# Two gated linear-attention blocks: the first four k chunks, and the transfers of x and of the first key weights, put in another order

## The chip, the core and the metric

The kernel runs on one core of a Trainium2 chip. The metric is the device time of one execution in microseconds (us), as the median of several runs. TensorE (PE) does the matmuls and the transposes, VectorE (DVE) and ScalarE (ACT) work on their results, GpSimd (POOL) builds masks, and SyncE (SP) issues most of the transfers from DRAM; ScalarE issues some.

## The reference

Two linear-attention blocks, A and B, read the same x (2048 x 640) with their own weights, and a gate mixes them:

```
g   = sigmoid((x * gate_w).sum(-1))
qkv = x @ wqkv                              # 640 x 1920, 32 heads of 20
phi = where(t > 0, t + 1, exp(t)) + 1e-6
kv  = sum over s of phi(k)[s] v[s]          # 20 x 20 for each head
o   = phi(q) kv / (phi(q) . sum phi(k))
out = g * (oA @ woA) + (1 - g) * (oB @ woB)
```

## The kernel before

x is worked in 16 chunks of 128 rows. The model dimension of 640 is five row blocks of 128 (c = 0 to 4). A **k chunk** is phi(k) for one chunk of x: for each of two halves of 320 columns, five matmuls (one for each c) add up in PSUM; the stationary operand is the chunk of x transposed (`xT[:, c, chunk]`), the moving one is row block c of the key weights (`wkA`). `k_done` then runs `phi` (L188): exp on ScalarE, two steps on VectorE, the result in `pk`. A **q block** (`q_block`, L244) is 20 matmuls of 512 columns with the query weights `wqA` stationary and xT moving, and phi again.

After the k chunks and q blocks of A come its gate, its sums over x and phi(k), its normalisation, then the same for B, and at last the products with the output weights. These stages lie behind the change and are not touched by it.

PSUM is four tiles (slots 0 to 3) that are used in turn; a tile can be written again when the work that reads it is done. `turn[0]` is the slot that comes next, unless a slot is named.

What decides the order at the start:

- Each engine takes its instructions in the order in which the program has them. TensorE begins with seven warm-up matmuls (L151) on constants.
- x chunks 0 to 3 come from DRAM as rows (`xn`) and are transposed on TensorE (`x_transpose`, L181: five transposes into PSUM, then one copy of 640 columns to `xT` on VectorE or ScalarE). The other twelve chunks come already transposed by 15 transposing loads on SP (L123), five for each group of four chunks.
- Loads are issued on two queues, SP's and ScalarE's. SP's has x chunk 0, row blocks 0, 2 and 4 of wkA, then wqA (one load of 800 KB, L119) and the transposing loads. ScalarE's has x chunk 1, row blocks 1 and 3 of wkA, then x chunks 2 and 3 in one load. A row block and an x chunk are 160 KB each.
- `k_first` (L216) does the first two k chunks side by side, block by block: transposes of chunks 0 and 1; blocks 0 and 1 for chunk 0, then for chunk 1 (8 matmuls); block 2 for both (4); block 3 for both (4); block 4 for chunk 0 (2); the transposes of chunks 2 and 3; block 4 for chunk 1 (2). Their sums lie in slots 2 and 3, and both phis are called at the end.
- The main loop (L636) goes on with k chunks 2 and 3 (slots 0 and 1, 10 matmuls each), the q blocks of the first 512 rows (slots 2 and 3), k chunks 4 to 7, and so on.

Of the kernel before, what the change touches and what calls it, by code (L numbers as in the profile page):

```python
# [8 lines left out]
P = 128  # L9
# [5 lines left out]
S, D, H = 2048, 640, 32  # L15
Dh = D // H
DT = D // P
ST = S // P
NB = 4
CB = 4  # L20
# [10 lines left out]
def kernel(  # L31
# [11 lines left out]
    nc = tc.nc  # L43
# [10 lines left out]
    turn = [0]  # L54

    def ps_raw(name, slot=None):

        if slot is None:
            slot = turn[0]
            turn[0] = (slot + 1) % 4  # L60
        return psum.tile([P, 4 * HB], BF16, tag=f"ps{slot}", name=name)

    def ps(name, slot=None):

        return ps_raw(name, slot).bitcast(FP32).rearrange("p (b n) -> p b n", b=2)

    xT = persist.tile([P, DT, S], BF16, name="xT")
# [27 lines left out]
    wq_dram = [A_wqkv.rearrange("(c p) f -> p c f", p=P), B_wqkv.rearrange("(c p) f -> p c f", p=P)]  # L95
# [7 lines left out]
    wk = [None, None]  # L103
# [3 lines left out]
    def load_x(eng, lo, hi):  # L107
        eng.dma_start(out=xn[:, lo:hi, :], in_=xb0[:, lo:hi, :])

    def load_wk(eng, c):  # L110
        eng.dma_start(out=wk[0][:, c, :], in_=wq_dram[0][:, c, D:2 * D])

    load_x(nc.sync, 0, 1)
    load_x(nc.scalar, 1, 2)
    for c in range(DT):
        load_wk(nc.scalar if c % 2 else nc.sync, c)
    load_x(nc.scalar, 2, 4)
    wq[0] = wpool.tile([P, DT, D], BF16, tag="wq", name="wqA")
    nc.sync.dma_start(out=wq[0][:], in_=wq_dram[0][:, :, 0:D])  # L119
# [1 line left out]
    for n in range(1, NB):  # L121
        for c in range(DT):
            nc.sync.dma_start_transpose(  # L123
                out=xT[:, c, n * HB:(n + 1) * HB], in_=x2[n * HB:(n + 1) * HB, c * P:(c + 1) * P]
# [8 lines left out]
    for sign, base in ((1, 0), (-1, Dh - 1)):  # L133
        nc.gpsimd.affine_select(
            out=maskE[:], in_=maskE[:], pattern=[[sign * P, DT], [-sign * Dh, H]],
# [3 lines left out]
    for r in range(4):  # L139
        rows = slice(32 * r, 32 * r + 32)  # L140
        for sign, base in ((1, 0), (-1, Dh - 1)):
            nc.gpsimd.affine_select(
                out=E4[rows], in_=E4[rows], pattern=[[sign, D]],
# [34 lines left out]
            nc.scalar.activation(out=ge[b][:], in_=pt[:, 0, :], func=ACT.Exp, scale=(-1.0, 1.0)[b])  # L178
            nc.vector.tensor_scalar(ge[b][:], ge[b][:], 1.0, 1e30, op0=ALU.add, op1=ALU.min)

    def x_transpose(i, slot, eng):  # L181
        pt = ps_raw("xt", slot)
        for c in range(DT):
            nc.tensor.transpose(out=pt[:, c * P:(c + 1) * P], in_=xn[:, i, c * P:(c + 1) * P], identity=ident[:])
        copy = nc.scalar.copy if eng == "act" else nc.vector.tensor_copy
        copy(out=xT[:, :, i * P:(i + 1) * P], in_=pt[:, 0:D].rearrange("p (c n) -> p c n", c=DT))

    def phi(dst, src, n, lifted=False):  # L188

        e = work.tile([P, 2, n], BF16, tag="e", name="e", bufs=3)  # L190
        nc.scalar.activation(out=e[:], in_=src, func=ACT.Exp)  # L191
        if lifted:
            nc.scalar.activation(out=dst, in_=src, func=ACT.Identity, bias=lift[:])
        nc.vector.tensor_scalar(e[:], e[:], 1.0, EPS, op0=ALU.min, op1=ALU.add)  # L194
        if lifted:
            nc.vector.tensor_tensor(out=dst, in0=dst, in1=e[:], op=ALU.max)
            return
        nc.vector.scalar_tensor_tensor(out=dst, in0=src, scalar=1.0 + EPS, in1=e[:], op0=ALU.add, op1=ALU.max)  # L198

    def k_mm(b, i, c, pt, hf):  # L200
        nc.tensor.matmul(  # L201
            pt[:, hf, 0:HF], lhsT=xT[:, c, i * P:(i + 1) * P], rhs=wk[b][:, c, hf * HF:(hf + 1) * HF],
            start=(c == 0), stop=(c == DT - 1),
        )

    def k_done(b, i, pt):
        phi(pk[:, i, :].rearrange("p (b n) -> p b n", b=2), pt[:, :, 0:HF], HF)

    def k_chunk(b, i):
        pt = ps(f"k{'AB'[b]}")  # L210
        for hf in range(2):
            for c in range(DT):
                k_mm(b, i, c, pt, hf)
        k_done(b, i, pt)

    def k_first():  # L216

        for i in range(2):
            x_transpose(i, i, "dve")
        pts = [ps("kA", 2 + i) for i in range(2)]  # L220
        for cs in ((0, 1), (2,), (3,), (4,)):
            for i in range(2):
                for c in cs:
                    for hf in range(2):
                        k_mm(0, i, c, pts[i], hf)
                if cs[0] == DT - 1 and i == 0:
                    x_transpose(2, 0, "dve")
                    x_transpose(3, 1, "act")
        for i in range(2):
            k_done(0, i, pts[i])  # L230

    def q_unit(b, m, h, lifted=False):
# [11 lines left out]
    def q_block(b, m, n):  # L244

        pt = ps(f"q{'AB'[b]}")
        for u in range(2):
            for c in range(DT):
                nc.tensor.matmul(  # L249
                    pt[:, u, :], lhsT=wq[b][:, c, (m + u) * P:(m + u + 1) * P], rhs=xT[:, c, n * HB:(n + 1) * HB],  # L250
                    start=(c == 0), stop=(c == DT - 1),
                )
        phi(pqT[b][:, m:m + 2, n * HB:(n + 1) * HB], pt, HB)
# [378 lines left out]


    k_first()
    turn[0] = 0
    for n in range(2):  # L636
        for i in range(max(2, n * CB), (n + 1) * CB):
            k_chunk(0, i)
        for m in (0, 2):
            q_block(0, m, n)  # L640
# [3 lines left out]
    for n in range(1, NB):  # L644
        nc.sync.dma_start(
            out=xn[:, n * CB:(n + 1) * CB, :], in_=x2[n * HB:(n + 1) * HB, :].rearrange("(q p) d -> p q d", p=P)
# [36 lines left out]
    with tc.manual_schedule():  # L683
# [15 lines left out]
        with late_pool("single") as single:  # L699
            halves = [[bank(single, f"s{c}{hf}") for hf in range(2)] for c in (3, 4)]  # L700
            for c in (3, 4):
                pts = [t[:, 0:HF] for t in halves[c - 3]]
# [16 lines left out]
        for i in range(1, half):  # L719
            p, after = pairs[i], pairs[i + 1] if i + 1 < half else None  # L720
# [45 lines left out]
```

## Time and profile before

| | us |
|---|---|
| median of 3 runs | 197.63 |
| lowest and highest | 197.43, 198.44 |
| the profiled execution | 198.14 |
| its span in the profile | 196.4 |
| first k matmul (L201) starts | 5.11 |
| first q matmul (L249) starts | 12.40 |
| TensorE work of the chain ends | 190.09 |

Busy times of the page are shares of the span; a wait is the idle time of an engine before an instruction, and the name behind the arrow is what ended it. Times on the timeline and in the chain are from the span's start. A time to landing counts from the issue of a transfer until the data is there. PEld is the loading of the stationary operand, which goes on beside matmuls.

### The profile page before, as it was taken

Reading aid. Unit: us, or ns where it says so; the run is one execution under the profiler, and the core shown is the slowest. Engines: PE = TensorE matmul, PEld = TensorE weight load, DVE = VectorE, ACT = ScalarE, POOL = GpSimd, SP = SyncE. Lnnn points to the kernel's source line nnn. Section 1 sums busy time; section 2 is a strip of 40 time slices with the busy share of each in tenths; the row PEclk is TensorE's granted clock in tenths of the full one; section 3 lists DMA queues with packets and bytes.
Section 4 is the critical chain, followed back from the end, with each engine's and each line's share of the span. In section 5 each row is a group of like instructions: output and inputs, shape, how many; then the busy total and the mean of one; then the engine's idle time right before and its main releaser. Section 6 shows DMA issues by size and latency. Waiting matters only on the chain.

```text
span 196.4 us, 3665 instructions
## 1 busy us (share of the span) xinstructions
PE 190.9 (97%) x1513; PEld 122.4 (62%) x1520; DVE 148.8 (76%) x240; ACT 82.4 (42%) x110; POOL 9.3 (5%) x23
## 2 busy tenths in 40 slices
PE   8899999999999999999999999999999999999992
PEld 3456547664476666877764444576667777777771
DVE  4296868898989896888787677768779798885553
ACT  2245455555941874366652554413552520122110
POOL 7920000000000000000000000000000000000000
PEclk9999999999999999999999999999999999999999
DMA  6975469970050000220071000000000002122112
GB/s 174 313 143 83 104 163 373 246 199 4 2 167 3 0 0 3 77 90 3 0 155 38 2 0 0 0 3 0 3 0 0 3 0 100 71 82 78 72 68 69
DMA packets 18189, 14.21 MB, mean 72 GB/s; under 512 B 8782, under 2 KB 18046, under 8 KB 18174
## 3 DMA queue, kind: packets, MB, share of 16 engines
q1 hardware_dynamic: 17566, 13.17, 25.1%
q10 hardware_dynamic: 576, 0.82, 1.2%
q8 instruction: 12, 0.20, 0.4%
q14 instruction: 3, 0.02, 0.1%
q0 software_dynamic: 32, 0.00, 0.0%
HBM read 9.40 MB, written 2.62 MB: 61 GB/s over the span
## 4 chain that ended last, share of the span: by engine, by line
PE 93%; DMA 3%; DVE 1%; issue 0%; SPq 0%; ACT 0%; DVEq 0%; ACTq 0%
PE gB L271 11%; PE kB L201 11%; PE qB L238 11%; PE kA L201 11%; PE gs L297 8%; PE qA L238 7%; PE ox L501 6%; PE oy L501 5%; PE oz L501 5%; PE qA L249 4%; DMA wkA<-in_A_wqkv_dram 3%; PE ow L501 2%; PE gA L271 2%; PE mA L414 1%; DVE osb L506 1%; PE exA L474 1%
## 5 line engine op out<-in xcount | busy, mean ns | idle before, releaser
L201 PEld LDWEIGHTS <-xT 128*128 128x128 bf16 x320 | 30.8, 98 | 14.0 <-issue 1.3
L194 DVE TENSOR_SCALAR e<-e 128x640 bf16<-128x640 bf16 (+1 forms) x52 | 19.2, 369 | 11.1 <-ACT e L191 10.0
L201 PE MATMUL kA<-wkA,xT 128*128 128x320 bf16 x160 | 23.1, 299 | 0.7 <-DMA wkA<-in_A_wqkv_dram 0.6
L271 PEld LDWEIGHTS <-xn 128*128 128x128 bf16 x192 | 18.3, 98 | 8.4 <-issue 1.3
L271 PE MATMUL gB<-pk,xn 128*128 128x320 bf16 x160 | 22.9, 299 | 0.0
L201 PE MATMUL kB<-wkB,xT 128*128 128x320 bf16 x160 | 22.9, 299 | 0.0
L238 PE MATMUL qB<-xT,wqB 128*128 128x512 bf16 x97 | 21.9, 379 | 0.2
L191 ACT ACTIVATE e<-kA 128x640 bf16<-128x640 f32 x16 | 11.3, 704 | 13.5 <-PE kA L201 13.5
L238 PEld LDWEIGHTS <-wqB 128*128 128x128 bf16 x100 | 9.6, 98 | 11.4 <-issue 0.3
L191 ACT ACTIVATE e<-kB 128x640 bf16<-128x640 f32 x16 | 11.3, 705 | 10.7 <-PE kB L201 10.7
L191 ACT ACTIVATE e<-qB 128x1024 bf16<-128x1024 f32 x10 | 10.2, 1024 | 13.1 <-PE qB L238 10.7
L198 DVE SCALAR_TENSOR_TENSOR pk<-kA,e 128x640 bf16<-128x640 f32 x16 | 13.2, 825 | 1.9 <-PE gps L157 0.5
L191 ACT ACTIVATE e<-qA 128x1024 bf16<-128x1024 f32 x10 | 10.2, 1024 | 10.5 <-PE qA L249 5.2
L198 DVE SCALAR_TENSOR_TENSOR pk<-kB,e 128x640 bf16<-128x640 f32 x16 | 13.2, 824 | 1.7
L238 PE MATMUL qA<-xT,wqA 128*128 128x512 bf16 x58 | 13.5, 379 | 0.1
L198 DVE SCALAR_TENSOR_TENSOR pqTB<-qB,e 128x1024 bf16<-128x1024 f32 x10 | 12.2, 1225 | 1.0
L535 ACT COPY u<-ox 128x320 f32<-128x320 f32 x8 | 3.4, 427 | 20.9 <-PE ox L501 20.9
L488 ACT CAST ex<-exA 128x1024 bf16<-128x1024 f32 x10 | 9.6, 1017 | 5.8 <-PE exA L474 4.9
L501 PEld LDWEIGHTS <-xT 128*128 128x128 bf16 x85 | 8.1, 98 | 2.9
L238 PEld LDWEIGHTS <-wqA 128*128 128x128 bf16 x60 | 5.7, 97 | 6.7 <-issue 0.3
L501 PEld LDWEIGHTS <-pqTA 128*128 128x128 bf16 x85 | 8.0, 98 | 2.9
L501 PEld LDWEIGHTS <-pqTB 128*128 128x128 bf16 x80 | 7.8, 98 | 3.0
(118 smaller groups left out, 272.5 us busy)
## 6 DMA issues: line engine op xcount, KB each, us to landing
out_dram<-osb SPq DMA_DIRECT2D x15, 160.0 KB, 1.8
xn<-in_A_x_dram SPq DMA_DIRECT2D x3, 640.0 KB, 5.9
wqA<-in_A_wqkv_dram SPq DMA_DIRECT2D x1, 800.0 KB, 6.8
wvA<-in_A_wqkv_dram SPq DMA_DIRECT2D x1, 800.0 KB, 9.7
wkB<-in_B_wqkv_dram SPq DMA_DIRECT2D x1, 800.0 KB, 4.7
wqB<-in_B_wqkv_dram SPq DMA_DIRECT2D x1, 800.0 KB, 4.8
wvB<-in_B_wqkv_dram SPq DMA_DIRECT2D x1, 800.0 KB, 5.0
woA<-in_A_wo_dram SPq DMA_DIRECT2D x1, 750.0 KB, 12.2
```

What stands on the lines that cost most here:

```text
L191: nc.scalar.activation(out=e[:], in_=src, func=ACT.Exp)
L194: nc.vector.tensor_scalar(e[:], e[:], 1.0, EPS, op0=ALU.min, op1=ALU.add)
L198: nc.vector.scalar_tensor_tensor(out=dst, in0=src, scalar=1.0 + EPS, in1=e[:], op0=ALU.add, op1=ALU.max)
L201: nc.tensor.matmul(pt[:, hf, 0:HF], lhsT=xT[:, c, i * P:(i + 1) * P], rhs=wk[b][:, c, hf * HF:(hf + 1) * HF], start=(c == 0), stop=(c == D ...
L238: nc.tensor.matmul(pt[:, u, :], lhsT=wq[b][:, c, m * P:(m + 1) * P], rhs=xT[:, c, n * HB:(n + 1) * HB], start=(c == 0), stop=(c == DT - 1),)
L249: nc.tensor.matmul(pt[:, u, :], lhsT=wq[b][:, c, (m + u) * P:(m + u + 1) * P], rhs=xT[:, c, n * HB:(n + 1) * HB], start=(c == 0), stop=(c ...
L271: nc.tensor.matmul(pt[:, hf, 0:HF], lhsT=xn[:, i, c * P:(c + 1) * P], rhs=pk[:, i, hf * HF:(hf + 1) * HF], start=(i == 0), stop=(i == ST - 1),
L297: nc.tensor.matmul(pt[:, n, 0:HF], lhsT=left[:, i, n * P:(n + 1) * P], rhs=right[:, i, :], start=(first and i == 0), stop=(i == hc - 1), s ...
L414: nc.tensor.matmul(dst, lhsT=KVT[:rows, j, c * P:(c + 1) * P], rhs=wo_sb[b][:rows, j, hf * HF:(hf + 1) * HF], start=(k == 0), stop=(k == 1),)
L488: nc.scalar.copy(out=ex[:], in_=src)
L501: nc.tensor.matmul(dst, lhsT=left[:, c, r0:r0 + P], rhs=right[:, c, :], start=(first and c == 0), stop=(c == DT - 1), skip_group_check=not ...
L535: nc.scalar.copy(out=self.u2[:], in_=self.at("x"))
```

## The change

wkA's row blocks 2, 3 and 4 come in one transfer of 480 KB on SP's queue; ScalarE's queue has x chunk 1, row block 1 and then x chunks 2 and 3. `x_transpose` can copy to xT in pieces; chunks 0 and 1 are copied as blocks 0 and 1, then blocks 2 to 4. `k_first` does four chunks: blocks 0 and 1 for chunks 0 and 1; the transposes of chunks 2 and 3; block 2 for chunks 0 and 1; blocks 0 and 1 for chunks 2 and 3 (slots 0 and 1); then, chunk by chunk, the blocks that are left, each chunk followed by its phi. The main loop skips the first four chunks and starts with the q blocks in slot 2, as before.

```
-    def load_wk(eng, c):
-        eng.dma_start(out=wk[0][:, c, :], in_=wq_dram[0][:, c, D:2 * D])
+    def load_wk(eng, lo, hi):
+        eng.dma_start(out=wk[0][:, lo:hi, :], in_=wq_dram[0][:, lo:hi, D:2 * D])
 
     load_x(nc.sync, 0, 1)
     load_x(nc.scalar, 1, 2)
-    for c in range(DT):
-        load_wk(nc.scalar if c % 2 else nc.sync, c)
+    load_wk(nc.sync, 0, 1)
+    load_wk(nc.scalar, 1, 2)
+    load_wk(nc.sync, 2, DT)
     load_x(nc.scalar, 2, 4)
...
-    def x_transpose(i, slot, eng):
+    def x_transpose(i, slot, eng, cuts=(0, DT)):
...
-        copy(out=xT[:, :, i * P:(i + 1) * P], in_=pt[:, 0:D].rearrange("p (c n) -> p c n", c=DT))
+        src = pt[:, 0:D].rearrange("p (c n) -> p c n", c=DT)
+        for lo, hi in zip(cuts, cuts[1:]):
+            copy(out=xT[:, lo:hi, i * P:(i + 1) * P], in_=src[:, lo:hi])
...
     def k_first():
 
+        pts = [ps("kA", (2 + i) % 4) for i in (0, 1)]
+
+        def part(i, cs):
+            for c in cs:
+                for hf in range(2):
+                    k_mm(0, i, c, pts[i], hf)
+
         for i in range(2):
-            x_transpose(i, i, "dve")
-        pts = [ps("kA", 2 + i) for i in range(2)]
-        for cs in ((0, 1), (2,), (3,), (4,)):
-            for i in range(2):
-                for c in cs:
-                    for hf in range(2):
-                        k_mm(0, i, c, pts[i], hf)
-                if cs[0] == DT - 1 and i == 0:
-                    x_transpose(2, 0, "dve")
-                    x_transpose(3, 1, "act")
+            x_transpose(i, i, "dve", (0, 2, DT))
         for i in range(2):
+            part(i, (0, 1))
+        x_transpose(2, 0, "dve")
+        x_transpose(3, 1, "act")
+        for i in range(2):
+            part(i, (2,))
+        pts += [ps("kA", i) for i in (0, 1)]
+        for i in (2, 3):
+            part(i, (0, 1))
+        for i in range(4):
+            part(i, (3, 4) if i < 2 else (2, 3, 4))
             k_done(0, i, pts[i])
...
     k_first()
-    turn[0] = 0
+    turn[0] = 2
     for n in range(2):
-        for i in range(max(2, n * CB), (n + 1) * CB):
+        for i in range(CB if n else 0, CB * 2 * n):
             k_chunk(0, i)
```

## The prediction

> **What bounds the kernel now.** I read the page first (busy shares, then the chain that ended last), then the chain in order of time for the first 13 us, then the timeline, the DMA issues and the DMA queues of that stretch. On the page TensorE is busy 97% of the span, and the chain that ended last is 93% TensorE; the one other entry of size is a load.
>
> ```profile
> PE 190.9 (97%) x1513; PEld 122.4 (62%) x1520; DVE 148.8 (76%) x240; ACT 82.4 (42%) x110; POOL 9.3 (5%) x23
> PE 93%; DMA 3%; DVE 1%; issue 0%; SPq 0%; ACT 0%; DVEq 0%; ACTq 0%
> ```
>
> So the end is set by TensorE's stream, and only the time in which TensorE stands still can be won. The chain in order of time shows where that is (start, length, what):
>
> ```profile
> 1.72 5.23 DMA wkA<-in_A_wqkv_dram
> 6.95 0.04 issue
> 7.00 0.70 PE kA L201 x4
> 7.70 0.02 issue
> 7.72 0.97 PE kA L201 x6
> 8.69 0.68 PE xt L184 x10
> 9.37 0.29 PE kA L201 x2
> 9.66 0.02 issue
> 9.68 2.89 PE kA L201 x20
> 12.57 0.22 PE qA L249
> 12.78 0.05 issue
> 12.84 4.05 PE qA L249 x18
> 16.89 5.43 PE kA L201 x40
> ```
>
> wkA's row block 2 lands at 1.72 + 5.23 = 6.95, and from then on the chain is TensorE without a break until the last microseconds. A k matmul costs 5.43 / 40 = 0.136 us; 20 of them cost 2.72 plus 0.16 for the last one to run out (299 ns on the page, less 0.136), which is the 2.89 of the row. The timeline gives the stretch before 6.95 and the waits inside it:
>
> ```profile
> 5.11 1.26 PE L201 MATMUL kA<-wkA,xT 128*128 128x320 bf16 x8
> 7.00 1.70 PE L201 MATMUL kA<-wkA,xT 128*128 128x320 bf16 x10 [0.62 <-DMA wkA<-in_A_wqkv_dram]
> 8.63 0.56 PEld L184 LDWEIGHTS <-xn 128*128 128x128 bf16 x10 [0.28 <-DMA xn<-in_A_x_dram]
> 9.21 3.36 PE L201 MATMUL kA<-wkA,xT 128*128 128x320 bf16 x22
> 12.40 4.48 PE L249 MATMUL qA<-xT,wqA 128*128 128x512 bf16 x19
> ```
>
> Eight matmuls (row blocks 0 and 1, x chunks 0 and 1) start at 5.11; at 0.136 TensorE could take the next at 6.20. The first q matmul starts at 12.40. Between lie 32 matmuls (32 x 0.136 = 4.35) and 10 transposes (0.68): 5.03 us of work in 6.20 us. So **1.17 us** of standing still is all that this change can win: 0.59% of 197.63.
>
> **When data lands.** From issue times and times to landing of single transfers: x chunk 0 at 3.7, x1 at 3.9, row blocks 0 and 1 at 4.6 and 4.7, block 2 at 6.95, block 3 at 7.6, block 4 at 8.2, x chunks 2 and 3 (one transfer) at 8.6. All of them are 1440 KB, and the two queues (q1 holds SP's transfers, q10 ScalarE's) are never empty until then. The answers for 6 to 7 us and 7 to 8 us (packets, MB, share):
>
> ```profile
> q10 hardware_dynamic: 94, 0.19, 51.6%
> q1 hardware_dynamic: 97, 0.11, 39.3%
> ...
> q1 hardware_dynamic: 254, 0.32, 87.1%
> q10 hardware_dynamic: 34, 0.07, 17.0%
> ```
>
> While both have work they move about equally many packets (97 and 94 here; 153 and 162 from 3 to 4 us), and when one runs dry the other gets nearly all. Bytes moved come to 1429 KB at 7.0 us, so the mean engine has everything by then; but the last landings are 8.2 and 8.6, so the slowest engine is over 1 us behind. Landings, not means, are what TensorE waits for.
>
> **The change, part by part.**
>
> *Transfers.* SP issues x0, block 0, then blocks 2 to 4 as one 480 KB transfer; ScalarE issues x1, block 1, then x2 and x3. Bytes are the same, issues are 6 in place of 8. An issue is 0.39 to 0.46 us, so x2 and x3 are issued at 1.7 in place of 2.2; that alone is worth nothing, since q10 holds x1 and block 1 until about 4.7. What counts is that they move one block (160 KB) ahead in q10. Landings in q10 were 480 KB at 7.6 and 800 KB at 8.6; 640 KB lies between, at 8.1 by bytes and, with 448 packets (128 for each 160 KB load; 192 of the 576 are left for x2 and x3) between 384 and 576, at 7.95 by packets. I take **x2 and x3 at 8.0** (bounds: 7.3, a third of a us under block 3's landing, and 8.6, where they land now). Blocks 2 to 4 can be used only when all 480 KB are there. All 1440 KB had landed at 8.6, with 160 KB or more of wqA already mixed in; 8.2 is block 4's landing. I take **8.5** (bounds 7.5 and 9.0). So block 2 comes 1.5 us later for TensorE than now.
>
> *Order on TensorE.* After the first eight matmuls the queue holds the ten transposes of chunks 2 and 3, then four matmuls of block 2 (chunks 0 and 1), eight of blocks 0 and 1 for chunks 2 and 3, then 8 and 12 more, each chunk's phi after its last. TensorE takes them in order, so everything waits behind the transposes, and these behind x2 and x3. Transposes: 8.0 + 0.05 to 8.73 (0.68). Block 2's matmuls wait for the later of 8.73 and 8.5 + 0.05, so start at 8.73. Then 32 matmuls, 4.35, and q starts at 13.08 in place of 12.40: **+0.68 us**. The rule to keep: the later of (x2/x3 + 0.73) and (blocks 2 to 4 + 0.05), plus 4.35; it breaks even at 8.05. Now TensorE fills the wait for x2 and x3 with ten matmuls of blocks 2 to 4; in the change it stands from 6.20 to 8.05.
>
> *Copies to xT.* Chunks 0 and 1 are copied in two pieces (256 and 384 columns) in place of one of 640 (0.49). A second instruction adds nothing at the least and, at most, another 0.49 each; a 128x1 memset of 0.06 is the nearest row for a bare instruction. Either is hidden: DVE has nothing from 5.6 to 9.13, and TensorE's eight matmuls gate nothing before 8.0. Chunk 2's copy ends at 8.0 + 0.05 + 0.34 + 0.2 + 0.49 = 9.1, before its first matmul at 8.73 + 0.55 = 9.28; chunk 3's on ScalarE (0.69) ends at 9.5, before 9.8. Both hold with 0.2 to 0.3 to spare, and move along with x2 and x3.
>
> *Four phis at the end.* phi of chunk 0 now starts 16 matmuls (2.2 us) before q, and q's first block takes the same PSUM tile (slot 2). In the profile that phi took from 8.69 to 10.71, 2.02 us: the tile is free 0.2 us ahead. With a slow first DVE step (0.66 in place of 0.32, as one was) q waits 0.15. I count 0, and 0.2 in the upper end. The second tile is needed 2.2 us later and is free 1 us after q starts.
>
> *SP's queue.* wqA is issued at 3.91 after a wait of 1.3 us for the landing of x0; with two transfers fewer ahead it may go at 2.2, and the transposing loads with it. It stands behind blocks 2 to 4 in q1. wqA lands 1.6 us before its use now, so 0 either way.
>
> Everything after q is a closed TensorE stream, so the 0.68 passes to the end. The profiled execution took 198.14 (span 196.4, 1.7 around it) and would take 198.8; the runs' median is 197.63, so I forecast 197.63 + 0.68 = **198.3**.
>
> **Rivals.**
>
> *Fewer, larger transfers move faster.* From 4 to 7 us the queues moved 226, 239 and 307 GB/s, from 7 to 9, with almost only wqA, 385 and 388. If the merged load ran at 385 from 4.0, the remaining 784 KB would take 2.04 in place of 3.0 us: landings about 0.9 earlier, x at 7.1 and blocks at 7.6. Start 7.83, q at 12.18, **197.4**. Against it: the share of engine time is 0.86 to 0.95 in that dip, so the engines were not short of work; and row blocks 0 and 1, in 160 KB pieces too, ran at 384 to 390. Chance 0.18. The Trainium skill, "DMA: Bandwidth & Descriptors", section Bandwidth, speaks for this rival: it advises batching transfers to 1 MiB or more. The rows of 3.25 to 3.75 us (384 and 390 GB/s with 160 KB loads) do not show such a need here.
>
> *x2 and x3 land no earlier.* If the lag of the slowest engine and not the place in q10 sets their landing, it stays at 8.6: start 9.33, q at 13.68, +1.28, **198.9**. It decides from a landing of 8.3 on (start 9.04, +0.99, 0.5%). For it: blocks 2 and 3 landed 0.7 apart though each was third in its queue, so landings hang on lag as much as on place. Chance 0.22. This ends slower.
>
> *TensorE's rate falls in the longer gap.* The seven warm-up matmuls (512 columns) start 0.43 apart, while ten q matmuls of that width take 2.16: at the start TensorE runs at half the rate, and by 5.11 at full (0.136 per k matmul). The gap now is 0.8 us and leaves the rate alone; the change makes it 1.85 us. If half rate came back and lasted as at the start (0.85 to about 4.8, some 4 us), it would cost 2 us more: **200.3**. No row shows a gap of that length. Chance 0.05. The Trainium skill, "TensorE: Matmul & The Clock Gate", Part 1, has the clock halved after about one idle window of 3.4 us, by which this gap is too short; its section "A second HAM failure mode: psum-queue depth-cycling" tells of shorter idles that did it.
>
> *The whole gap closes* (x and blocks by 6.4): -1.17, **196.5**. Nothing landed in that order before 7.6. Chance 0.04.
>
> **How the numbers follow.** Forecast 0.51, the rivals 0.18, 0.22, 0.05 and 0.04. Half a per cent (0.99 us) is about what a measurement of this kernel can tell from no change. Within it lie the forecast (less 0.03 for its tail) and the first rival: 0.66. Slower: 0.22 + 0.05 + 0.03 = 0.30; faster: 0.04. The range takes in the first two rivals and the 0.2 of the phi with a little for the scatter of medians: 197.2 to 199.2; the half-rate case and the closed gap are left out.
>
> **What would show it.** The chain should hold the load of xn in place of wkA's; the transposes of chunks 2 and 3 should start near 8.05 with TensorE idle before them by some 1.8 us; block 2's matmuls should follow at once (if they wait, blocks 2 to 4 came after 8.7); the first q matmul near 13.1; k matmuls at 0.136 after the gap. I am wrong if x2 and x3 land before 7.3 (then the change gains), if the first landings (3.7 to 4.7) move because wqA is issued earlier, or if q waits for phi by more than 0.2.

## The result, and the profile after

The changed kernel takes 198.97 us (median of 22 runs, 197.34 to 201.86), the kernel before 197.66 (22 runs, 197.05 to 198.44). The ratio is 1.0049, 95% interval 1.0035 to 1.0064: slower by half a per cent, +0.97 us. Five of the 22 runs (200.62 to 201.86) had a mean granted TensorE clock of 0.991 where the others had 0.996 to 1.000, and the comparison leaves them out, though they belong to what the change costs: the median of the other 17 is 198.66, none of the 22 runs of the kernel before is above 198.44, and over all runs the medians differ by 1.31 us. The trace of experiment 1 shows where such a run loses its time.

The profiled execution took 198.05 us, so it is among the shorter ones of a kernel that scatters by over 2 us. Its page, busy shares and then the chain that ended last by engine:

```profile
PE 190.4 (97%) x1520; PEld 122.1 (62%) x1520; DVE 148.7 (76%) x242; ACT 82.5 (42%) x110; POOL 9.2 (5%) x23
PE 93%; DMA 3%; DVE 1%; ACTq 0%; ACT 0%; issue 0%; DVEq 0%
```

Seen from the page nothing has changed. The chain in order of time (start, length, what) shows the new bound:

```profile
1.73 5.53 DMA xn<-in_A_x_dram
7.26 0.05 issue
7.31 0.73 PE xt L185 x10
8.04 4.35 PE kA L204 x32
12.39 4.32 PE qA L260 x20
```

The load in the chain is now x chunks 2 and 3 in place of wkA's block 2; it lands at 7.26. The ten transposes follow, then all 32 remaining k matmuls without a break, then the q block. The timeline of the same execution (start, length, instruction, idle before and its end):

```profile
4.73 1.26 PE L204 MATMUL kA<-wkA,xT 128*128 128x320 bf16 x8
7.31 0.73 PE L185 MATMUL xt<-ident,xn 128*128 128x128 bf16 x10 [1.32 <-DMA xn<-in_A_x_dram]
7.88 4.51 PE L204 MATMUL kA<-wkA,xT 128*128 128x320 bf16 x32
12.23 4.48 PE L260 MATMUL qA<-xT,wqA 128*128 128x512 bf16 x20
```

q starts at 12.23, in the kernel before at 12.40: this execution is even 0.2 us shorter in its span (196.2 against 196.4). Here the trace of the kernel before misleads too: its execution took 198.14, 0.48 above the median of that kernel. A second trace of the changed kernel (199.08 us, experiment 8) is nearer to what most runs look like. Its chain, then two rows of its timeline:

```profile
1.73 6.40 DMA xn<-in_A_x_dram
8.13 0.05 issue
8.18 0.73 PE xt L185 x10
8.91 4.50 PE kA L204 x32
13.41 4.32 PE qA L260 x20
```

```profile
8.18 0.73 PE L185 MATMUL xt<-ident,xn 128*128 128x128 bf16 x10 [2.09 <-DMA xn<-in_A_x_dram]
13.24 1.03 PE L260 MATMUL qA<-xT,wqA 128*128 128x512 bf16 x4
```

Here x chunks 2 and 3 land at 8.13, the 480 KB of wkA at 8.86 (issued at 1.73), and q starts at 13.24 on the timeline, 0.84 later than before, with a span of 197.2, 0.8 longer. Both executions are one kernel; only the landing differs. That the start of q carries to the end shows in the other traces: q at 11.45, 11.83, 12.40, 13.36 (experiments 7 and 5, the kernel before, experiment 3) goes with spans of 195.5, 195.8, 196.4, 197.3. In experiments 6 and 11 alone the span is 0.5 longer than q's start (12.59 and 15.90) would make it. There TensorE's chain ends at 190.27 and 193.58, 0.2 and 3.5 after that of before, as it should; the rest comes behind it.

The packed traces also hold when each of the 16 parts of a load landed; a load is there when the last one is. For the 480 KB load and for the last of three separate loads, row block 4, in experiments 5 and 9:

| trace | load | half of the parts by | the last part at |
|---|---|---|---|
| the change, first | 480 KB | 6.6 | 7.28 |
| the change, second | 480 KB | 6.8 | 8.86 |
| experiment 1 | 480 KB | 6.7 | 8.84 |
| experiment 3 | 480 KB | 6.6 | 8.98 |
| experiment 6 | 480 KB | 6.7 | 8.20 |
| experiment 11 | 480 KB | 6.8 | 10.03 |
| experiment 5 | block 4 | 6.9 | 7.66 |
| experiment 9 | block 4 | 6.7 | 7.87 |

Half of the merged load is there as early as half of block 4; what differs is the last few parts. In experiment 1 fourteen of the 16 had landed by 6.75 and the last two came at 8.53 and 8.84; of x chunks 2 and 3 fourteen had landed by 5.78, and the last two came at 7.65 and 7.95. TensorE waits for such a tail.

### The profile page after: what moved, and what is told of

It reads as the page before. It is cut to its first block, busy times and chain, and to the rows that moved or that the text cites. A ratio compares the mean times of both kernels' runs of the same rounds, so it can differ in the third digit from the quotient of the medians.

```text
span 196.2 us, 3673 instructions
## 1 busy us (share of the span) xinstructions
PE 190.4 (97%) x1520; PEld 122.1 (62%) x1520; DVE 148.7 (76%) x242; ACT 82.5 (42%) x110; POOL 9.2 (5%) x23
## 4 chain that ended last, share of the span: by engine, by line
PE 93%; DMA 3%; DVE 1%; ACTq 0%; ACT 0%; issue 0%; DVEq 0%
PE gB L282 11%; PE kB L204 11%; PE qB L249 11%; PE kA L204 11%; PE gs L308 8%; PE qA L249 7%; PE ox L512 6%; PE oy L512 5%; PE oz L512 5%; PE qA L260 4%; DMA xn<-in_A_x_dram 3%; PE ow L512 2%; PE gA L282 2%; PE mA L425 1%; DVE osb L517 1%; PE exA L485 1%
## 5 line engine op out<-in xcount | busy, mean ns | idle before, releaser
L197 DVE TENSOR_SCALAR e<-e 128x640 bf16<-128x640 bf16 (+1 forms) x52 | 19.3, 371 | 11.9 <-ACT e L194 11.0
L204 PE MATMUL kA<-wkA,xT 128*128 128x320 bf16 x160 | 22.6, 299 | 0.1
```

What stands on the lines that cost most here:

```text
L204: nc.tensor.matmul(pt[:, hf, 0:HF], lhsT=xT[:, c, i * P:(i + 1) * P], rhs=wk[b][:, c, hf * HF:(hf + 1) * HF], start=(c == 0), stop=(c == D ...
```

## The experiments

**1. The transfers alone.**

```
+    load_wk(nc.sync, 0, 1)
+    load_wk(nc.scalar, 1, 2)
+    load_wk(nc.sync, 2, DT)
     load_x(nc.scalar, 2, 4)      # k_first, x_transpose and the main loop as before
```

> Transfers of the change (x1, row block 1, x2/x3 on ScalarE; blocks 2 to 4 as one on SP), order of TensorE as before. Theory A (TensorE stands still until the last of one late landing, and nothing else is ready; any order that waits for blocks 2 to 4 or x2/x3 pays): TensorE waits from 6.2 for the 480 KB; with a landing of 8.2 (median of the change, worked back from +1.0 us) and 5.03 us of work behind it q starts near 13.3, +0.8 us, ratio 1.004, with a scatter between runs of over 1 us, and some runs at a granted clock near 0.991. Rival B (the new order is the cost, transposes ahead of the matmuls): within 0.3 us of before, ratio 0.999 to 1.001.

Measured: 199.15 us (197.91 to 201.41, 12 runs), ratio 1.0067 (1.0038 to 1.0095). Theory A's size and scatter; rival B, that the new order alone is the cost, is out, for the order here is the old one. Three of the 12 runs were at 0.991, and the profiled one (201.34) is among them. Its timeline, then its stretches of 1 us (the columns after the length are the busy times of PE, PEld, DVE, ACT and POOL with counts, the granted TensorE clock, the share of the DMA engines, GB/s):

```profile
8.88 2.83 PE L202 MATMUL kA<-wkA,xT 128*128 128x320 bf16 x10 [2.37 <-DMA wkA<-in_A_wqkv_dram]
11.51 0.95 PE L185 MATMUL xt<-ident,xn 128*128 128x128 bf16 x10
```

```profile
7.00:8.00 1.00, 0.00 (x0) 0.00 (x0) 0.00 (x0) 0.00 (x0) 0.87 (x2) 1.00 1.00 351
8.00:9.00 1.00, 0.12 (x1) 0.10 (x1) 0.00 (x0) 0.00 (x0) 0.93 (x2) 0.78 1.67 355
9.00:10.00 1.00, 1.00 (x5) 0.54 (x4) 0.00 (x0) 0.00 (x0) 0.94 (x2) 0.50 2.20 98
10.00:11.00 1.00, 1.00 (x6) 0.52 (x5) 0.00 (x0) 0.00 (x0) 0.94 (x2) 0.50 0.40 90
11.00:12.00 1.00, 1.00 (x8) 0.76 (x7) 0.00 (x0) 0.25 (x1) 0.06 (x1) 0.51 1.34 261
12.00:13.00 1.00, 0.96 (x12) 0.59 (x10) 0.75 (x3) 0.96 (x2) 0.00 (x0) 1.00 0.74 154
```

The merged load lands at 8.84. TensorE had stood still for 2.37 us, and 2.05 us into that gap, at 8.56, the granted clock fell to 0.50, to come back at 11.97. Ten k matmuls take 2.83 in place of 1.52. The half rate lasted 3.41 us, the first 0.3 of them idle, and cost some 1.4: from the first matmul after the gap to q are 6.61 us, in experiment 4 5.22. The Trainium skill, "TensorE: Matmul & The Clock Gate", Part 1, has full rate come back after about 3.4 us of sustained work and the clock fall after about one idle window of 3.4 us. The length of the half rate agrees with that; the idle window does not describe this gap, which had lasted 2.05 us when the clock fell.

**2. The order alone.** The load lines of before in the changed kernel:

```
-    load_wk(nc.sync, 2, DT)
+    for c in range(DT):
+        load_wk(nc.scalar if c % 2 else nc.sync, c)
```

> Order of TensorE and the split copies of the change, transfers as before (five row blocks apart, x2/x3 fourth on ScalarE's queue). Theory A: the transposes stand ahead of everything and wait for x2/x3, which land at 8.6 as before, so q starts near 13.7: +1.3 us, ratio 1.0065, again with wide scatter and some runs near a granted clock of 0.991. Rival C (the merged transfer is the cost): blocks land as before, ratio about 1.000.

Measured: 198.41 us (198.07 to 198.81, 9 runs), ratio 1.0043 (1.0025 to 1.0061). Between the two: with these transfers the order alone costs 0.86 us, with the wait where theory A has it, on x chunks 2 and 3:

```profile
7.67 0.73 PE L184 MATMUL xt<-ident,xn 128*128 128x128 bf16 x10 [0.63 <-DMA xn<-in_A_x_dram]
8.24 4.51 PE L203 MATMUL kA<-wkA,xT 128*128 128x320 bf16 x32
12.59 1.67 PE L259 MATMUL qA<-xT,wqA 128*128 128x512 bf16 x7
```

They landed at 7.63 and not at 8.6. The wait before them is only 0.63 because the first eight k matmuls took 2.13 us in this trace (4.91 to 7.04) in place of 1.26. But the scatter is gone (0.74 us, and no run at 0.991), which theory A had not said: the scatter belongs to the transfers.

**3. Something for TensorE to do in the gap.**

```
             part(i, (0, 1))
+        fill = ps("fill", 0)
+        for k in range(5):
+            nc.tensor.matmul(fill[:, 0, :], lhsT=one_l, rhs=one_r, start=True, stop=True)
         x_transpose(2, 0, "dve")
```

> The changed kernel with five more matmuls of constants (512 columns, result unused, 1.1 us in all) after the first eight k matmuls, where TensorE stands still. Theory A with the clock (the gap of 1.3 us and more makes the clock fall in about one run of five): no run at 0.991, none above 200; the other runs as in the change, ratio 1.003 to 1.006. Rival D (the runs above 200.5 us come from something else than the gap): one run in five still above 200 at a granted clock near 0.991. If the fill itself ends after the landing it costs up to 0.2 us.

Measured: 198.91 us (198.22 to 200.23, 9 runs), ratio 1.0067 (1.0043 to 1.0091). No run at 0.991, as theory A has it, with 9 runs too few to prove it alone (at 5 in 22 nine would show none one time in ten). One run of 200.23 had a clock of 0.997, so a late landing alone can go that far. In its trace x2 and x3 landed at 8.34 and the merged load at 8.98.

**4. The kernel before, a second trace.**

> The kernel before, unchanged, for a second trace of its transfers. Theory A: the rate of the transfers between 4 and 7 us differs from one execution to the next (226 to 307 GB/s in the first trace, 384 in that of the changed kernel), so this trace may show either; landings of x2/x3 between 7.3 and 8.8 with q starting at 12.0 to 12.5 all the same. Rival C (wqA and the transposing loads, issued at 3.9 to 4.4, cause the dip): the dip from 4 us on is there again, as in any trace in which wqA is issued at 3.9.

Measured: one run of 198.63. Block 2 landed at 7.03, x2 and x3 at 8.4, q started at 12.29, and the dip was there: 290 and 192 GB/s from 4 to 6 us. It was also there in experiment 2 (206 from 5 to 6), where wqA goes out at 3.9 too, so this trace leaves rival C standing; experiment 6 goes on with it.

**5. Three loads in place of one.**

```
-    load_wk(nc.sync, 2, DT)
+    for c in range(2, DT):
+        load_wk(nc.sync, c, c + 1)
```

> The changed kernel with row blocks 2, 3 and 4 as three transfers of 160 KB on SP in place of one (wqA then also goes out only at 3.9 again, when x0 has landed). Theory A: the order costs what it cost with the old transfers (+0.43%), the scatter of the change (197.3 to 199.7, and 200.6 to 201.9 with the clock at 0.991) comes with the new transfers. If the single 480 KB transfer or the early wqA makes the scatter, it goes here: median 198.2 to 198.5, highest under 199.2, no run at 0.991, ratio about 1.004. If it comes from x2/x3 being third in ScalarE's queue with three blocks on SP, it stays: over 1.5 us between runs, some runs at 0.991.

Measured: 197.85 us (197.33 to 198.36, 12 runs), ratio 1.0014 (1.0000 to 1.0029). The scatter is 1.0 us (in the change 2.3 without the runs at 0.991, 4.5 with them), no run is at 0.991, and the time falls by more than expected. Its timeline:

```profile
4.91 1.26 PE L205 MATMUL kA<-wkA,xT 128*128 128x320 bf16 x8
6.91 0.73 PE L186 MATMUL xt<-ident,xn 128*128 128x128 bf16 x10 [0.74 <-DMA xn<-in_A_x_dram]
11.83 2.54 PE L261 MATMUL qA<-xT,wqA 128*128 128x512 bf16 x11
```

x chunks 2 and 3 landed at 6.87. They are issued at the same time and on the same queue as in the change, where they landed at 7.26 and 8.13. wqA, too, goes out later here (3.94 in place of 2.20), so the experiment changes two things; experiment 6 parts them.

**6. wqA held back, the merged load kept.**

```
+    hold = [persist.tile([1, P], BF16, name=f"hold{k}") for k in range(2)]
+    for k in range(2):
+        nc.sync.dma_start(out=hold[k][:], in_=gate_w.rearrange("(o f) -> o f", o=1)[:, 0:P])
     nc.sync.dma_start(out=wq[0][:], in_=wq_dram[0][:, :, 0:D])
```

> The changed kernel, its 480 KB transfer kept, with two tiny loads of 256 B (not used) on SP ahead of wqA, so that wqA and the transposing loads wait for x0 and are issued at 3.9 as before. If the early issue of wqA and the transposing loads makes the landings late and scattered, this goes back to 198.2 to 198.5 with under 0.8 us of scatter. If the single 480 KB transfer does it, it stays as in the change: ratio 1.005, over 1.5 us between runs, some runs at a granted clock near 0.991.

Measured: 199.96 us (198.66 to 201.70, 6 runs, one at 0.991), ratio 1.0099 (1.0067 to 1.0130). wqA was issued at 3.96, as in experiment 5, and nothing got better: the early issue of wqA is not the cause, the merged load is. It even got worse than the change (1.0035 to 1.0064), which nothing here explains; the two tiny loads are the only other edit. wqA's data still moves beside the merged load from 4 us on, so whether the load would be late with nothing beside it is not tested. The trace also has no dip (368, 373 and 373 GB/s from 4 to 7 us), so an issue of wqA at 3.9 does not bring rival C's dip by itself.

**7. x first, and all work that can be done with blocks 0 and 1.** Three transfers on each queue before block 2, every block apart, and eight more matmuls ahead of block 2:

```
+    load_x(nc.sync, 2, 3)
+    load_x(nc.scalar, 3, 4)
+    load_wk(nc.sync, 2, 3)
+    load_wk(nc.scalar, 3, 4)
+    load_wk(nc.sync, 4, 5)
...
+        x_transpose(2, 0, "dve", (0, 2, DT))
         x_transpose(3, 1, "act")
         pts += [ps("kA", i) for i in (0, 1)]
         for i in (2, 3):
             part(i, (0, 1))
+        for i in range(2):
+            part(i, (2,))
```

> x2 on SP and x3 on ScalarE as third in each queue, then blocks 2, 3, 4 apart; TensorE does blocks 0 and 1 for all four chunks, then block 2 and the rest. Theory A (what lands third decides, and work must be there for it): x2 and x3 land at 6.0 to 7.6, the gap before the transposes is 0.2 to 1.2 us, block 2 is there (8.2 at the latest) when 8 more matmuls are done, q starts between 11.7 and 12.4: -0.7 to 0 us, ratio 0.996 to 1.000, scatter under 1 us, no run at 0.991. Rival E (the copies or phi of four chunks close together bound the stretch): q blocks wait for phi, ratio 1.001 or more.

Measured: 197.16 us (196.90 to 197.59, 12 runs), ratio 0.9977 (0.9965 to 0.9990): faster than the kernel before, and the least scatter of all. Its timeline:

```profile
4.86 1.26 PE L207 MATMUL kA<-wkA,xT 128*128 128x320 bf16 x8
6.18 0.73 PE L188 MATMUL xt<-ident,xn 128*128 128x128 bf16 x10
7.04 4.51 PE L207 MATMUL kA<-wkA,xT 128*128 128x320 bf16 x32
11.45 2.75 PE L263 MATMUL qA<-xT,wqA 128*128 128x512 bf16 x12
```

TensorE's gaps before q are 0.2 to 0.3 us now; x2 and x3 land at 6.1 and 6.4 (issued near 1.7, 4.4 and 4.6 to landing). Rival E is out: q follows the last k matmul.

**8. The changed kernel again.**

> The changed kernel again for a second trace. Theory A: x2/x3 land somewhere between 7.2 and 9.5 and q starts 5.1 us after that landing, whatever it is.

Measured: one run of 199.08, the second trace of the section above. From the landing at 8.13 to q at 13.24 are 5.11 us, as expected; in the first trace 4.97.

**9. Three loads with the old order.**

```
+    load_wk(nc.sync, 0)
+    load_wk(nc.scalar, 1)
+    for c in range(2, DT):
+        load_wk(nc.sync, c)
     load_x(nc.scalar, 2, 4)      # the rest as before
```

> Blocks 2, 3, 4 as three loads on SP and x2/x3 third on ScalarE (as with three loads and the new order, ratio 1.0014), TensorE's order as before. Theory F (the merged transfer makes the landings late; the new order costs something by itself because the transposes stand ahead): block 2 lands near 5.9, block 3 near 6.9, block 4 near 7.3, x2/x3 by 7.5, so TensorE waits little and q starts 11.6 to 12.1: ratio 0.996 to 0.999, scatter under 1.2 us. Rival H (the order is free once x2/x3 is third; only landings count): as with the new order, ratio 1.000 to 1.003.

Measured: 198.28 us (197.90 to 199.11, 12 runs), ratio 1.0039 (1.0020 to 1.0058). Both theories missed: with these transfers the old order is the slower one (1.0039 against 1.0014 in experiment 5; the intervals overlap a little). The profiled run was the shortest of the 12 (q at 12.03), so what the others waited for is not in a trace. The kernel has blocks 2 to 4 one behind the other on one queue and needs all three before the transposes, where the new order needs x2 and x3; that would explain it, and is not shown.

**10. Blocks 3 and 4 merged.**

```
-    load_wk(nc.sync, 2, DT)
+    load_wk(nc.sync, 2, 3)
+    load_wk(nc.sync, 3, DT)
```

> The changed kernel with block 2 as one load and blocks 3 and 4 as one of 320 KB. Theory F by size: half way, ratio 1.002 to 1.004, scatter 1 to 1.5 us. If only the full merge hurts: as three loads, ratio 1.000 to 1.002. If any merge over row blocks hurts: as the change, ratio 1.005, runs above 199.5.

Measured: 198.73 us (197.59 to 200.85, 12 runs, two at 0.991), ratio 1.0033 (1.0012 to 1.0055). Half way, as theory F by size has it: three loads 1.0014, two 1.0033, one 1.0049. The intervals of neighbours overlap.

**11. The merged load on ScalarE's queue.**

```
-    load_wk(nc.sync, 2, DT)
-    load_x(nc.scalar, 2, 4)
+    load_wk(nc.scalar, 2, DT)
+    load_x(nc.sync, 2, 4)
```

> The changed kernel with the 480 KB transfer on ScalarE's queue and x2/x3 on SP's, ahead of wqA. Theory F (the shape of the merged transfer): still late and scattered, ratio 1.004 to 1.010, over 1.5 us between runs. Rival G (what stands behind it on SP's queue, wqA and the transposing loads, delays it): blocks land by 7.5, ratio 0.999 to 1.002, scatter under 1 us.

Measured: 202.13 us (200.21 to 203.66, 6 runs, five at 0.991 or below), ratio 1.0197 (1.0157 to 1.0237). This ratio counts four of the runs at 0.991; the one run at full clock took 200.21, 2.4 us more than the kernel before. Later still: the merged load lands at 10.03, with nothing behind it on its queue, so rival G is out. The timeline of the wait:

```profile
7.31 0.73 PE L185 MATMUL xt<-ident,xn 128*128 128x128 bf16 x10 [0.47 <-DMA xn<-in_A_x_dram]
10.07 4.22 PE L204 MATMUL kA<-wkA,xT 128*128 128x320 bf16 x19 [2.03 <-DMA wkA<-in_A_wqkv_dram]
```

The queues from 7 to 8 and from 8 to 9 us (packets, MB, share; q10 holds the merged load):

```profile
q1 hardware_dynamic: 261, 0.33, 92.1%
q10 hardware_dynamic: 31, 0.04, 11.0%
...
q1 hardware_dynamic: 528, 0.29, 260.1%
q10 hardware_dynamic: 18, 0.02, 5.9%
```

From 7 to 9 us the merged load moves 31 and 18 packets a microsecond while SP's queue moves hundreds. Twelve of its 16 parts had landed by 7.11; the other four came at 7.57, 8.15, 8.90 and 10.03. It is late by a small tail. The core as a whole was still moving 371 and 313 GB/s, so total bandwidth was not short; what holds up these parts is not shown.

**12. The merged load in two halves by partitions.**

```
+    for h in range(2):
+        rows = slice(64 * h, 64 * h + 64)
+        nc.sync.dma_start(out=wk[0][rows, 2:DT, :], in_=wq_dram[0][rows, 2:DT, D:2 * D])
```

> The changed kernel with the 480 KB transfer cut in two by partitions (0 to 63 and 64 to 127), each with three rows of 1280 B a partition. If the three rows of a partition in one transfer make it late: as the change, ratio 1.004 to 1.008, over 1.5 us between runs. If the length of one transfer does: smaller, ratio 1.000 to 1.003, scatter under 1.2 us.

Measured: 201.65 us (199.99 to 202.15, 6 runs, four at 0.991), ratio 1.0174 (1.0133 to 1.0216), the runs at 0.991 counted; the two at full clock took 199.99 and 200.02. It does not decide between the two causes: these transfers moved only 210, 227 and 206 GB/s from 6 to 9 us at full engine share (1.05 to 1.11), less than any other trace in that stretch, which is another effect on top. Its trace is one of the two at full clock, in spite of two waits with only transposes between them:

```profile
7.48 0.73 PE L187 MATMUL xt<-ident,xn 128*128 128x128 bf16 x10 [1.31 <-DMA xn<-in_A_x_dram]
9.68 4.52 PE L206 MATMUL kA<-wkA,xT 128*128 128x320 bf16 x32 [1.46 <-DMA wkA<-in_A_wqkv_dram]
```

## Why the prediction was right, point by point

The sign was right and the path too: +0.97 us was measured where +0.68 was forecast, and TensorE waits for x chunks 2 and 3. The sizes behind it were less good than the sum, and they partly cancel.

- **TensorE's start sets the end; at most 1.17 us to win.** Right as a path: q's start moved the span one for one in every trace but those of experiments 6 and 11, and the best kernel (experiment 7) started q at 11.45, 0.22 above the floor of 11.23. But 1.17 and 12.40 are those of one execution of 198.14. The median before is 197.66, which by the same rule puts q near 11.9 and leaves some 0.7 to win; experiment 7 won 0.45 of it. By the same estimate the median of the change without the runs at 0.991, 198.66, puts its q near 12.8, between the two traces (12.23 at 198.05, 13.24 at 199.08). So the forecast had q 0.25 too late in the change (13.08) and 0.5 too late in the kernel before (12.40), and the difference came out a third too small.
- **The order puts x2 and x3 ahead of everything.** Right. The chain has the load of xn in place of wkA's. TensorE stands still for 1.3 and 2.1 us in the two traces before the transposes (forecast 1.85). Block 2's matmuls follow the transposes at once in the first trace; in the second they wait another 0.15 for the merged load.
- **x2 and x3 at 8.0, blocks at 8.5, q at 13.08.** In the second trace 8.13, 8.86 and 13.24; in the first 7.26, 7.28 and 12.23. The rule (the later of x2/x3 + 0.73 and blocks + 0.05, then 4.35) gives 13.26 and 12.34 from these landings; in the first trace the matmuls begin 0.57 after the transposes and not 0.68. A landing before 7.3 was a sign of being wrong, with a gain: the first trace has it, with 7.26 and a span 0.2 shorter than that of before, but the median run does not. (The 1429 and 784 KB of the prediction are of 1000 bytes, its 1440 of 1024; that shifts these sums by under 0.1 us.)
- **Why 8.0 came out about right was luck.** The prediction took it from the place in ScalarE's queue alone. With that place and three loads beside it, x2 and x3 landed at 6.87 and 7.09 (the traces of experiments 5 and 9; the median run of experiment 5 is 0.14 longer than its trace, which puts it near 7.0), under its bound of 7.3; the merged load, which it priced at nothing, put them later again.
- **Copies, phi and SP's queue at nothing.** Right. The split copies let the first k matmul start at 4.73 to 4.83 in place of 5.11, which the gap swallows. phi of chunk 0 is done at 12.17 in the first trace and q starts at 12.23, so that margin is thin. wqA went out at 2.20 and landed by 11.0, two us before its use; holding it back (experiment 6) gained nothing.
- **The merged load.** Here is the part that was sized wrongly. I weighed the merge as neutral or, in the first rival, as a gain of 0.9 us in landings. The first trace is that rival to the letter (379 GB/s from 5 to 8 us, q at 12.23 where it has 12.18), but other executions are not (275 to 306 from 4 to 7 in the second), and over the runs the landings become later and scatter, those of x2 and x3 beside it too; in experiment 6 at 368 to 373 GB/s the merged load still landed only at 8.2. Against three loads with the same order it costs 0.35% (1.0049 against 1.0014), which is most of the slowdown. The advice of the Trainium skill, "DMA: Bandwidth & Descriptors", section Bandwidth, to batch transfers did not pay here: with three loads of 160 KB the data that TensorE waited for was there earlier. Why the last parts of the merged load come so late stays open. It goes with the load's own shape or size (experiments 5, 10 and 11), not with its queue and not with the early issue of wqA.
- **The order alone** costs 0.43% with the old transfers, where x2 and x3 are fourth in ScalarE's queue. Where they are third the new order is no dearer than the old: 1.0049 against 1.0067 with the merged load, 1.0014 against 1.0039 with three loads, though the intervals of each pair overlap. Its price follows the landing of x2 and x3.
- **The half-rate rival** had 0.05 and came in 5 of 22 runs, at about the forecast price of 2 us (the runs at 0.991 have a median of 200.97, the other 17 of 198.66: 2.3, of which the half rate itself is some 1.4 by experiment 1's trace; the rest would be the later landing that brings it).
- **The call of no clear change** was near the edge: 0.49%, interval 0.35 to 0.64, where the prediction drew the line at 0.5.

## What to carry to other kernels

When several loads start a kernel, ask of each order what is left to do if the load at the head of the queue comes a microsecond late; the order before and that of experiment 7 had an answer, the change had none. Keep a load that something waits for in pieces that can be used as they land, and judge a merge by landings in several traces, not by GB/s in one. One profiled execution of a kernel that scatters can show a faster start than the kernel it is slower than: look at the times of all runs before reading it.

## What the runs showed of the hardware

- A gap on TensorE of 2.37 us brought the granted clock to 0.50, 2.05 us into it and for 3.41 us, in experiment 1. In experiment 11 it fell from 9.71 to 13.12, also 3.41 us, where transposes from 7.31 to 8.04 stood in the middle of the idle time and did not prevent it. A gap of 2.09 us in the second trace of the change did not bring it, nor did waits of 1.31 and 1.46 with the transposes between them in experiment 12, so the length of the wait alone does not decide.
- The first eight k matmuls took 1.26 us in ten of the 14 traces and 1.64, 1.92 and 2.13 in experiments 3, 11 and 2. The traces' record of the full clock begins at 5.73, 6.30 and 6.73 there, and at 3.88 to 5.14 in the ten: the moment at which TensorE reaches its full rate differs between these executions by up to 2.85 us. (In experiment 9, where block 2's matmuls follow without a break, it begins at 6.27.)
- One load of three row blocks landed, in all but one trace, later than three loads of the same bytes on the same queue (its last part at 7.28, 8.20, 8.84, 8.86 and 8.98; 7.66 and 7.87 for the last of three), with half of its parts there at about the same time, 6.6 to 6.9. The transfer on the other queue landed later beside it, too: x2 and x3 at 7.26, 7.55, 7.95, 8.13 and 8.34 in five traces, at 6.87 and 7.09 beside three loads.
